# Placing lookup tables on chip, or loading them whole: the tables of the second step of a Fourier-and-MLP kernel

## The chip, the cores and the metric

The kernel runs on one core of one Trainium2 chip. The metric is the device time of one execution in microseconds (us), lower is better. The engines are TensorE (PE; its weight loads are PEld), VectorE (DVE), ScalarE (ACT), GpSimd (POOL) and SyncE (SP, which here only issues transfers). All times inside an execution count from the start of its span. All executions quoted are of the state "fast"; there was no slow one.

## The reference, cut to what matters

```python
X = np.fft.rfft(x, axis=1)                 # x: 8 x 3008 x 256
Yr = Xr @ w_r - Xi @ w_i + b_r ;  Yi = Xr @ w_i + Xi @ w_r + b_i
Yr, Yi = soft_threshold(Yr, 0.01), soft_threshold(Yi, 0.01)
y = np.fft.irfft(Yr + 1j * Yi, n=3008, axis=1)
h = np.maximum(y.reshape(-1, 256) @ w_in, 0.0)        # 256 -> 2048
out = (s * h * h + b) @ w_out                         # 2048 -> 256
```

The transform of length 3008 = 94 x 32 is done as two DFT steps, each a matrix product with a table. The second step takes 24 pairs of frequencies, each with its own 128 x 128 block-structured table: `F_t` and `F_2` forward (for the real and imaginary part of the mixed input), `T_t` inverse.

## The kernel before

The kernel first takes batch 0 through the transform alone; after that it runs the MLP of one batch beside the transform of the next, and TensorE is full (10.00 busy in 80 to 90 us). The change touches batch 0 only. There, half of each table is zero, so the tables arrive compact (`F_c`, `T_c`), the full tiles are zeroed, and VectorE and ScalarE copy the blocks into place.

```python
H = NPAIR // 2                     # 12 of 24 pairs
F_c = uspool.tile([P, NPAIR, 2, N2], F16)          # compact forward tables
T_c = uspool.tile([P, NPAIR, 64], F16)             # compact inverse table

def emit_load_forward():           # issued early in the input's loading
    nc.sync.dma_start(out=F_c[:, 0:H], in_=F_d[:, 0:H]); ...
def emit_load_inverse():           # issued when the input is nearly through
    nc.sync.dma_start(out=F_c[:, H:], in_=F_d[:, H:])
    t_load = nc.sync.dma_start(out=T_c, in_=T_d)
    ...                            # identity, last table, biases, scalars

nc.vector.memset(F_t, 0.0); nc.vector.memset(T_t, 0.0)
for f in F_2: nc.gpsimd.memset(f, 0.0)

def place_f(h):      # ScalarE: 2 copies of 64 x 768
    for a in range(2): nc.scalar.copy(out=blocks(F_t)[r, q, :, a], in_=F_c[r, q])
def place_f_2(h):    # VectorE: 4 operations of 64 x 384, two of them with a sign
    ...
def place_t(h):      # VectorE: 4 copies of 32 x 768
    for i in range(4): nc.vector.tensor_copy(out=T_t[r, q, c : c + 64], in_=T_c[r, q])

# ... first DFT step of batch 0 (products with x, evictions ut) ...
place_f(0); place_f_2(0)
gate = nc.gpsimd.tensor_copy(out=w_in_t[0][0:1, 0:1], in_=T_c[0:1, 0, 0:1])
# behind the gate on GpSimd: loads of batch 1's input, of w_in and of w_out
for i in range(2 * U + 2):         # U = 6; 12 steps, pipelined
    mix(...)        # TensorE x8, then eviction g (VectorE in 2 of 3 steps, ScalarE in 1)
    fwd_dft(...)    # TensorE x8 with F_t and F_2; m (ScalarE), then z (VectorE)
    inv_dft(...)    # TensorE x4 with T_t; eviction vt
    if i == 0: place_t(0)
    if i == 1: place_f(1)
    if i == 2: place_f_2(1)
    if i == 3: place_t(1)
```

A one-element memset ahead of each load holds the load back until the right eviction is done: in the trace the memset for `F_c` runs at 8.37 us, behind an eviction ut, and the load is issued at 8.48.

## Time and profile before

| | before |
|---|---|
| time | 851.64 us, median of 3 (851.37 to 852.25) |
| span of the profiled execution | 849.4 us |
| first forward product of batch 0 | 17.14 us |
| sixth forward product | 27.46 us |
| first product of the MLP (with `w_in`) | 49.59 us |
| from there to the end | 799.8 us |

The two ends of what follows, from the TensorE timeline:

```profile
17.14 0.22 PE L441 MATMUL psf<-g,F_t 128*128 128x128 f16 x1 [0.55 <-DVE g L420]
...
27.46 0.22 PE L441 MATMUL psf<-g,F_t 128*128 128x128 f16 x1
```

"First forward product" is the first TensorE product with `F_t`; each step makes eight such products with `F_t` and `F_2`. The time from the first to that of the sixth step is what I call **the stretch**: it holds the placing copies that the change removes (the first of them starts at 17.00, just before it), it is 10.32 us here, and TensorE's own work in it is about 8.0, an estimate that the prediction works out from the trace.

### The profile page before, as it was taken

To read this page: it belongs to the slowest core of one execution; us is meant where nothing else is said; L and a number is where in the kernel's file an instruction comes from. 1 tells how busy PE (TensorE), PEld (TensorE's weight loads), DVE (VectorE), ACT (ScalarE), POOL (GpSimd) and SP (SyncE) were. 2 spreads that over 40 slices of the span, in tenths; PEclk is the share of its full clock that TensorE was granted. 3 is DMA by queue.
4 is the path that set the end of the run, shared out by engine and by line. 5 is a ranking of instruction groups with operands and counts; after the bars stand their busy time and mean duration, and the time that the engine had idled before them with its cause. 6 is when DMAs were issued, how large, how long until landed. Compare 5 with 4: busy or idle time off the path is not lost.

```text
span 849.4 us, 17085 instructions
## 1 busy us (share of the span) xinstructions
PE 835.0 (98%) x6645; PEld 600.5 (71%) x6645; DVE 697.0 (82%) x1027; ACT 643.2 (76%) x856; POOL 46.6 (5%) x72
## 2 busy tenths in 40 slices
PE   8899999999999999999999999999999999999997
PEld 7757777777677766777677776777667777766765
DVE  6898987888888987888878888888977888776674
ACT  5898887787778787787777887787877787766673
POOL 5321000000000000000000000000000000000000
PEclk9999999999999999999999999999999999999999
DMA  7937457324761367324662247613354223411111
GB/s 165 161 104 162 108 148 185 101 76 100 177 186 54 92 159 184 109 78 103 171 177 65 74 106 199 172 40 92 100 156 118 62 79 98 112 33 38 38 44 50
DMA packets 105458, 95.07 MB, mean 112 GB/s; under 512 B 9510, under 2 KB 97578, under 8 KB 104034
## 3 DMA queue, kind: packets, MB, share of 16 engines
q1 hardware_dynamic: 98930, 79.57, 32.6%
q0 software_dynamic: 6448, 14.42, 10.7%
q8 instruction: 52, 0.85, 0.4%
q14 instruction: 28, 0.23, 0.1%
HBM read 52.54 MB, written 46.66 MB: 117 GB/s over the span
## 4 chain that ended last, share of the span: by engine, by line
PE 88%; DVE 4%; ACT 3%; DMA 2%; issue 1%; POOL 0%; SPq 0%; DVEq 0%; ACTq 0%; POOLq 0%
PE psa L832 36%; PE psh L761 36%; PE psf L627 4%; PE psf L562 2%; PE psf L613 2%; PE psf L598 2%; PE psf L657 2%; PE psf L710 2%; ACT rt L768 1%; DVE gt L775 1%; DMA x<-in_x_dram 1%; DMA out_dram<-ost 1%; PE psh L410 1%; ACT yt L160 0%; ACT vs L160 0%
## 5 line engine op out<-in xcount | busy, mean ns | idle before, releaser
L768 ACT ACTIVATE rt<-psh 128x1024 f32<-128x1024 f32 (+2 forms) x384 | 387.1, 1009 | 119.1 <-PE psh L761 117.7
L775 DVE TENSOR_TENSOR gt<-rt 128x1024 f16<-128x1024 f32 (+2 forms) x321 | 384.0, 1199 | 98.1 <-ACT rt L768 97.4
L832 PE MATMUL psa<-w_out_t,gt 128*128 128x256 f16 (+1 forms) x3024 | 454.3, 272 | 0.1
L832 PEld LDWEIGHTS <-gt 128*128 128x128 f16 (+1 forms) x3024 | 300.9, 101 | 187.2 <-issue 1.7
L761 PE MATMUL psh<-yt,w_in 128*128 128x512 f16 (+1 forms) x1344 | 396.7, 378 | 0.3 <-ACT rt L768 0.3
L761 PEld LDWEIGHTS <-w_in 128*128 128x128 f16 x1536 | 142.9, 98 | 27.4 <-issue 2.1
L842 DVE SCALAR_TENSOR_TENSOR ost<-psa,s_bc,bias_bc 128x512 f32<-128x512 f32 (+2 forms) x97 | 71.0, 732 | 8.3 <-PE psa L832 7.1
L772 ACT ACTIVATE gt<-rt 128x1024 f16<-128x1024 f32 (+2 forms) x63 | 66.2, 1050 | 1.0
L632 DVE TENSOR_TENSOR ring<-psf,s 128x512 f16<-128x512 f32 x84 | 57.5, 684 | 3.7 <-PE psf L627 2.9
L160 ACT CAST v<-psf 128x512 f16<-128x512 f32 x78 | 45.3, 582 | 18.7 <-PE psf L657 18.7
L160 ACT CAST xf<-psf 128x512 f16<-128x512 f32 x82 | 47.9, 585 | 10.9 <-PE psf L598 10.8
L160 ACT CAST u<-psf 96x512 f16<-96x512 f32 x77 | 44.5, 580 | 11.0 <-PE psf L562 10.7
L761 PE MATMUL psh<-tail,w_in 128*128 128x512 f16 (+1 forms) x192 | 52.1, 353 | 0.0
L627 PE MATMUL psf<-W_g,xf 128*128 128x256 f16 x336 | 50.4, 273 | 0.0
L160 ACT CAST yt<-psf 128x480 f16<-128x480 f32 (+2 forms) x75 | 38.1, 520 | 13.6 <-PE psf L710 13.6
L189 POOL DMA_DIRECT2D x<-in_x_dram x36 | 18.9, 530 | 429.3 <-PE psf L562 428.0
L562 PE MATMUL psf<-x,A_t 94*96 94x512 f16 x104 | 39.7, 381 | 1.7 <-ACT yt L160 0.5
L638 DVE TENSOR_TENSOR ring<-ring,high 128x512 f16<-128x512 f16 x84 | 35.5, 423 | 2.3
L639 DVE TENSOR_TENSOR ring<-ring 128x512 f16<-128x512 f16 x84 | 35.5, 422 | 1.9
L637 DVE TENSOR_TENSOR ring<-ring,low 128x512 f16<-128x512 f16 x84 | 35.4, 421 | 1.6
L627 PEld LDWEIGHTS <-xf 128*128 128x128 f16 x336 | 32.9, 98 | 3.8
L710 PE MATMUL psf<-C_t,vs 96*128 96x96 f16 x448 | 33.0, 205 | 0.1
(89 smaller groups left out, 501.9 us busy)
## 6 DMA issues: line engine op xcount, KB each, us to landing
out_dram<-ost SPq DMA_DIRECT2D x152, 128.0 KB
ud<-u SPq DMA_DIRECT2D x28, 384.0 KB
us<-ud SPq DMA_DIRECT2D x28, 384.0 KB
vd<-v SPq DMA_DIRECT2D x42, 256.0 KB
vs<-vd SPq DMA_DIRECT2D x14, 768.0 KB
x<-in_x_dram POOLq DMA_DIRECT2D x28, 376.0 KB, 5.9
ring<-ring SPq DMA_DIRECT2D x280, 32.0 KB
out_dram<-ost SPq DMA_DIRECT2D x16, 120.0 KB
```

The costliest lines, as they stand in the source:

```text
L160: return None, nc.scalar.copy(out=dst, in_=src)
L562: nc.tensor.matmul(ps[0:96, :], A_t[0:N1, :], x16[(b, c)][0:N1, j * D : (j + 2) * D], start=True, stop=True,)
L627: nc.tensor.matmul(ps[:, r, :], xt[:, 2 - r, dc], W_g[:, dc, r], start=(dc == 0), stop=(dc == DC - 1),)
L632: nc.vector.tensor_tensor(out=t, in0=ps, in1=hold[i // 2][:, i % 2].unsqueeze(1).to_broadcast([P, 2, D]), op=ALU.add,)
L638: nc.vector.tensor_tensor(out=m, in0=m, in1=high, op=ALU.min)
L710: nc.tensor.matmul(ps[:, j * 96 : (j + 1) * 96], vs[(b, h)][:, k, ec * P : (ec + 1) * P], C_t, start=True, stop=True,)
L761: nc.tensor.matmul(o, w_in_t[dc][:, mc * P : (mc + 1) * P], r, start=(dc == 0), stop=(dc == DC - 1),)
L768: nc.scalar.activation(out=rt[:, :, 0:w], in_=ps[:, :, 0:w], func=AF.Relu)
L772: nc.scalar.activation(out=gt[:, :, 0:w], in_=rt[:, :, 0:w], func=AF.Square)
L775: nc.vector.tensor_tensor(out=gt[:, :, 0:w], in0=rt[:, :, 0:w], in1=rt[:, :, 0:w], op=ALU.mult)
L832: nc.tensor.matmul(ps[0:size, h, :], gts[(ti, mc // 2)][:, mc % 2, sub * size : (sub + 1) * size], w_out_t[:, mc, :], start=(mc == 0), sto ...
L842: nc.vector.scalar_tensor_tensor(out=ost[0:size, 0:k], in0=ps[0:size, 0:k], scalar=s_bc[0:size], in1=bias_bc[0:size, 0:k], op0=ALU.mult, o ...
```

## The change

The intent is to take the copies off VectorE and ScalarE, where the first batch waits for them, and to let transfers bring the tables ready-made. It costs 983,040 more bytes. The first half of the forward tables is still placed, because it is needed first and the compact form is small.

```diff
-    F_d = nc.inline_tensor(fwd.astype(np.float16), name="dft_fwd").ap()
-    T_d = nc.inline_tensor(inv.astype(np.float16), name="dft_inv").ap()
+    F_d = nc.inline_tensor(fwd[:, 0:H].astype(np.float16), name="dft_fwd").ap()
+    ...                       # f_d, f_2_d, t_d: the same tables with their zeros, built beforehand
     def emit_load_inverse():
-        nc.sync.dma_start(out=F_c[:, H:].rearrange(...), in_=F_d[:, H:])
-        t_load = nc.sync.dma_start(out=T_c, in_=T_d)
+        nc.sync.dma_start(out=T_t[:, 0:H], in_=t_d[:, 0:H])
+        nc.sync.dma_start(out=F_t[:, H:], in_=f_d)
+        nc.sync.dma_start(out=F_2[1], in_=f_2_d)
+        t_load = nc.sync.dma_start(out=T_t[:, H:], in_=t_d[:, H:])
-    nc.vector.memset(F_t, 0.0)
-    nc.vector.memset(T_t, 0.0)
-    for f in F_2:
-        nc.gpsimd.memset(f, 0.0)
+    nc.vector.memset(F_t[:, 0:H], 0.0)
+    nc.gpsimd.memset(F_2[0], 0.0)
-        gate = nc.gpsimd.tensor_copy(out=w_in_t[0][0:1, 0:1], in_=T_c[0:1, 0, 0:1])
+        gate = nc.gpsimd.tensor_copy(out=w_in_t[0][0:1, 0:1], in_=F_t[0:1, H, 0:1])
-            if i == 0: place_t(0)      # (each behind the step's eviction g)
-            if i == 1: place_f(1)
-            if i == 2: place_f_2(1)
-            if i == 3: place_t(1)
```

More of the change, by code (lines that the diff above doesn't have):

```diff
@@ L123 @@
     A_d = nc.inline_tensor(first.astype(np.float16), name="dft_first").ap()
-    F_d = nc.inline_tensor(fwd.astype(np.float16), name="dft_fwd").ap()
-    T_d = nc.inline_tensor(inv.astype(np.float16), name="dft_inv").ap()
+    F_d = nc.inline_tensor(fwd[:, 0:H].astype(np.float16), name="dft_fwd").ap()
+    f_all = np.zeros((P, NPAIR, 2, 2, N2))
+    t_all = np.zeros((P, NPAIR, 2, 64))
+    for i in range(4):
+        r = slice(32 * i, 32 * i + 32)
+        f_all[r, :, :, i // 2] = fwd.reshape(P, NPAIR, 2, N2)[r]
+        t_all[r, :, i % 2] = inv[r]
+    f_2 = np.stack([-f_all[:, H:, 1], f_all[:, H:, 0]], axis=2)
+    f_d, f_2_d, t_d = (
+        nc.inline_tensor(t.reshape(P, -1, P).astype(np.float16), name=name).ap()
+        for t, name in ((f_all[:, H:], "fwd_rest"), (f_2, "fwd_rest_i"), (t_all, "dft_inv"))
+    )
     C_d = nc.inline_tensor(last.astype(np.float16), name="dft_last").ap()
@@ L220 @@
             nc.sync.dma_start(out=b_g[r : r + 1, i], in_=bv.unsqueeze(0))
-    F_c = uspool.tile([P, NPAIR, 2, N2], F16, name="F_c", tag="us")
+    F_c = uspool.tile([P, H, 2, N2], F16, name="F_c", tag="us")
+    F_2 = [uspool.tile([P, H, P], F16, name="F_2", tag="us") for _ in range(2)]
     b_h = cpool.tile([P, D], F16, name="b_h")
@@ L227 @@
     sel_t = cpool.tile([P, P], F16, name="sel_t")
-    T_c = uspool.tile([P, NPAIR, 64], F16, name="T_c", tag="us")
     eye_t = cpool.tile([P, P], F16, name="eye_t")
@@ L237 @@
     bb_bc = cpool.tile([P, 1], F32, name="bb_bc")
+    F_t = cpool.tile([P, NPAIR, P], F16, name="F_t")
+    T_t = cpool.tile([P, NPAIR, P], F16, name="T_t")
     def emit_load_forward():
         nc.sync.dma_start(
-            out=F_c[:, 0:H].rearrange("p q r k -> p q (r k)"), in_=F_d[:, 0:H]
+            out=F_c.rearrange("p q r k -> p q (r k)"), in_=F_d
         )
@@ L245, in emit_load_inverse @@
     def emit_load_inverse():
-        nc.sync.dma_start(
-            out=F_c[:, H:].rearrange("p q r k -> p q (r k)"), in_=F_d[:, H:]
-        )
-        t_load = nc.sync.dma_start(out=T_c, in_=T_d)
+        nc.sync.dma_start(out=T_t[:, 0:H], in_=t_d[:, 0:H])
+        nc.sync.dma_start(out=F_t[:, H:], in_=f_d)
+        nc.sync.dma_start(out=F_2[1], in_=f_2_d)
+        t_load = nc.sync.dma_start(out=T_t[:, H:], in_=t_d[:, H:])
         with tc.issue_after(t_load.ins):
@@ L271 @@
     nc.vector.memset(neg_lam, -LAM)
-    F_t = cpool.tile([P, NPAIR, P], F16, name="F_t")
-    nc.vector.memset(F_t, 0.0)
-    T_t = cpool.tile([P, NPAIR, P], F16, name="T_t")
-    nc.vector.memset(T_t, 0.0)
-    F_2 = [uspool.tile([P, H, P], F16, name="F_2", tag="us") for _ in range(2)]
-    for f in F_2:
-        nc.gpsimd.memset(f, 0.0)
+    nc.vector.memset(F_t[:, 0:H], 0.0)
+    nc.gpsimd.memset(F_2[0], 0.0)
     def make_bounds():
@@ L298, in place_w, with place_f, place_f_2 @@
             nc.scalar.copy(out=W_t[:, :, i], in_=w_st[i])
-    def place_f(h):
-        q = slice(h * H, h * H + H)
+    def place_f():
         for a in range(2):
             r = slice(64 * a, 64 * a + 64)
-            nc.scalar.copy(out=blocks(F_t)[r, q, :, a], in_=F_c[r, q])
-    def place_f_2(h):
-        q = slice(h * H, h * H + H)
+            nc.scalar.copy(out=blocks(F_t)[r, 0:H, :, a], in_=F_c[r])
+    def place_f_2():
         for a in range(2):
@@ L311, in place_f_2 @@
             nc.vector.tensor_scalar_mul(
-                out=blocks(F_2[h])[r, :, 0, a], in0=F_c[r, q, 1], scalar1=-1.0
+                out=blocks(F_2[0])[r, :, 0, a], in0=F_c[r, :, 1], scalar1=-1.0
             )
-            nc.vector.tensor_copy(out=blocks(F_2[h])[r, :, 1, a], in_=F_c[r, q, 0])
-    def place_t(h):
-        q = slice(h * H, h * H + H)
-        for i in range(4):
-            r = slice(32 * i, 32 * i + 32)
-            c = 64 * (i % 2)
-            nc.vector.tensor_copy(out=T_t[r, q, c : c + 64], in_=T_c[r, q])
+            nc.vector.tensor_copy(out=blocks(F_2[0])[r, :, 1, a], in_=F_c[r, :, 0])
     w_sum = cpool.tile([P, D], F16, name="w_sum")
@@ L382, in first_batch @@
                 with tc.issue_after(last_dve.ins):
-                    nc.vector.memset(F_c[0:1, H, 0, 0:1], 0.0)
-                    nc.vector.memset(T_c[0:1, 0, 0:1], 0.0)
+                    for t in (T_t[:, 0:H], F_t[:, H:], F_2[1], T_t[:, H:]):
+                        nc.vector.memset(t[0:1, 0, 0:1], 0.0)
                 emit_load_inverse()
@@ L389, in first_batch @@
         with tc.issue_after(last_dve.ins), tc.issue_after(last_act.ins):
-            place_f(0)
-            place_f_2(0)
-        gate = nc.gpsimd.tensor_copy(out=w_in_t[0][0:1, 0:1], in_=T_c[0:1, 0, 0:1])
+            place_f()
+            place_f_2()
+        gate = nc.gpsimd.tensor_copy(out=w_in_t[0][0:1, 0:1], in_=F_t[0:1, H, 0:1])
         with tc.issue_after(gate.ins):
@@ L402, in first_batch @@
         zt = {}
-        g_last = [None]
         def mix(ec, u):
@@ L416, in mix @@
             if u % 3 == 1:
-                g_last[0] = nc.scalar.copy(out=g, in_=ps)
+                nc.scalar.copy(out=g, in_=ps)
                 load["act"] += 1.02
             else:
-                g_last[0] = nc.vector.tensor_tensor(
+                nc.vector.tensor_tensor(
                     out=g, in0=ps,
@@ L523, in first_batch @@
                 some(3)
-            if i == 0:
-                with tc.issue_after(g_last[0].ins):
-                    place_t(0)
-            if i == 1:
-                with tc.issue_after(g_last[0].ins):
-                    place_f(1)
-            if i == 2:
-                with tc.issue_after(g_last[0].ins):
-                    place_f_2(1)
-            if i == 3:
-                with tc.issue_after(g_last[0].ins):
-                    place_t(1)
             if i == 9:
```

## The prediction

> **What bounds the kernel now.** I read the page's busy line first and then its chain of waits by engine.
>
> ```profile
> PE 835.0 (98%) x6645; PEld 600.5 (71%) x6645; DVE 697.0 (82%) x1027; ACT 643.2 (76%) x856; POOL 46.6 (5%) x72
> ...
> PE 88%; DVE 4%; ACT 3%; DMA 2%; issue 1%; POOL 0%; SPq 0%; DVEq 0%; ACTq 0%; POOLq 0%
> ```
>
> TensorE is the bound over the whole, and the 12% of the chain that is not TensorE is where a change off TensorE can act. The view by stretches (columns: PE, PEld, DVE, ACT, POOL busy us, clock, DMA share, GB/s) shows where that is.
>
> ```profile
> 10.00:20.00 10.00, 8.95 (x113) 7.84 (x111) 7.52 (x18) 8.19 (x14) 3.69 (x8) 0.90 0.70 162
> 20.00:30.00 10.00, 8.31 (x100) 6.72 (x98) 9.41 (x17) 7.44 (x12) 1.66 (x2) 1.00 1.04 205
> 30.00:40.00 10.00, 9.51 (x133) 8.46 (x131) 8.24 (x11) 8.53 (x15) 5.74 (x7) 1.00 1.04 158
> ...
> 80.00:90.00 10.00, 10.00 (x82) 7.59 (x81) 9.12 (x20) 9.14 (x14) 0.00 (x0) 1.00 0.33 87
> ```
>
> From about 57 us on TensorE is full. In the first batch it is not: in 20 to 30 us TensorE is idle for 1.7 us and VectorE is the fullest engine, 9.4 of 10. The tables of the second DFT step are placed just there, so this stretch decides. Next I read the timeline of VectorE in it.
>
> ```profile
> 15.86 1.22 DVE L420 TENSOR_TENSOR g<-psh,b_g 128x1024 f16<-128x1024 f32 x1 [0.26 <-PE psh L410]
> 17.00 1.52 DVE L321 COPY T_t<-T_c 32x768 f16<-32x768 f16 x4
> 18.66 1.23 DVE L420 TENSOR_TENSOR g<-psh,b_g 128x1024 f16<-128x1024 f32 x1
> 19.80 0.68 DVE L448 SCALAR_TENSOR_TENSOR z<-psf,m 128x512 f16<-128x512 f32 x1
> 20.68 0.69 DVE L448 SCALAR_TENSOR_TENSOR z<-psf,m 128x512 f16<-128x512 f32 x1 [0.20 <-ACT m L446]
> 21.29 0.45 DVE L311 TENSOR_SCALAR F<-F_c 64x384 f16<-64x384 f16 x1
> 21.66 0.23 DVE L314 COPY F<-F_c 64x384 f16<-64x384 f16 x1
> 21.91 0.26 DVE L311 TENSOR_SCALAR F<-F_c 64x384 f16<-64x384 f16 x1
> 22.09 0.26 DVE L314 COPY F<-F_c 64x384 f16<-64x384 f16 x1
> 22.38 1.23 DVE L420 TENSOR_TENSOR g<-psh,b_g 128x1024 f16<-128x1024 f32 x1
> 23.52 0.68 DVE L448 SCALAR_TENSOR_TENSOR z<-psf,m 128x512 f16<-128x512 f32 x1
> 24.11 1.44 DVE L321 COPY T_t<-T_c 32x768 f16<-32x768 f16 x4
> 25.58 0.69 DVE L448 SCALAR_TENSOR_TENSOR z<-psf,m 128x512 f16<-128x512 f32 x1
> ```
>
> The copies stand back to back with the evictions g and z that TensorE needs. On TensorE the timeline has the matching hole, a wait of 1.28 us for g, and on ScalarE two placing copies stand ahead of the activations m:
>
> ```profile
> 23.65 0.22 PE L441 MATMUL psf<-g,F_t 128*128 128x128 f16 x1 [1.28 <-DVE g L420]
> ...
> 17.66 0.83 ACT L304 COPY F_t<-F_c 64x768 f16<-64x768 f16 x1
> 18.40 0.68 ACT L446 ACTIVATE m<-psf,neg_lam 128x512 f32<-128x512 f32 x1
> 19.10 0.83 ACT L304 COPY F_t<-F_c 64x768 f16<-64x768 f16 x1
> 19.96 0.69 ACT L446 ACTIVATE m<-psf,neg_lam 128x512 f32<-128x512 f32 x1
> ```
>
> [...] The trace has 0.34 to 0.44 us for one, so I use the trace. [...] the trace reached 331 GB/s in 15 to 16 us, when these tables stream in. [...]
>
> **The change part by part.** Removed from VectorE: eight inverse-table copies (1.52 and 1.44 us) and four of the forward table (21.29 to 22.35, 1.06 us), together 4.0 us; also one and a half memsets of 1.34 us before 5 us, where VectorE waits for input anyway (1.05 us idle before the first eviction): worth nothing. Removed from ScalarE: two copies of 0.83 us. Removed from GpSimd: one of two memsets (2.71 us for both), done by 10.74, 4 us before use: worth nothing. Added: two 0.06 us gate memsets in a VectorE gap, and bytes. Before, half of F_c (196,608) and T_c (393,216) are 589,824 bytes; after, four transfers of 393,216 make 1,572,864: 983,040 more.
>
> What lies on the path, replaying the trace's durations:
> - Copies at 17.00: g before them ends at 17.08, and the next g needs a mix product that TensorE finishes at 18.62. They fill a wait; removal gives about 0.
> - ScalarE copies: without the second, m starts at 19.28, when its product is there, not 19.96. Its z then starts at 20.40, when the z before it lets VectorE go, not 20.68: 0.28 us.
> - Forward copies: g (22.38) then follows z directly, at 21.0: 1.06 plus 0.28 plus 0.04 = 1.38 us. The product after it moves from 23.65 to about 22.25.
> - Copies at 24.11: z (25.58) now waits not for them but for its m. The product ends at 22.9, but ScalarE is in the g of step 4 until about 23.2, so m runs 23.2 to 23.9 and z starts at about 23.9: 1.7 us early. So of these 1.44 us only 0.3 is new.
> - From there the line is full: the next g moves from 26.19 to about 24.5, the product of step 5 from 27.46 to about 25.7, that of step 6 from 29.18 to about 27.5. All are about 1.7 us earlier.
>
> Sum: 5.7 us of work leaves two engines, 1.7 us leaves the path. A floor checks it: TensorE's own work per step is 0.87 (mix) + 0.44 (forward) + 0.22 (inverse) + a third of 0.22, about 1.6 us, so the five steps from 17.14 to 27.46 (10.3 us) cannot fall below 8.0, and the gain cannot pass 2.3 us. Later work depends on the first batch and on transfers issued from it; after 57 us TensorE is full and keeps the lead. So 851.64 - 1.7 = 849.9, rounded to 849.8 because an order of VectorE that takes the first z ahead of g could gain a little more.
>
> **The rivals.** (1) The loads take the place of the copies: TensorE would wait for a table. The bytes of the present loads are through near 16.0 us (244 GB/s in 14 to 15, 331 in 15 to 16) and the gate that waits for them runs here:
>
> ```profile
> 16.72 0.18 POOL L393 COPY w_in<-T_c 1x1 f16<-1x1 f16 x1 [5.97 <-DMA T_c<-dft_inv]
> ```
>
> That is 0.7 us for completion. At 331 GB/s, as estimates from those rows, the four new loads land at about 16.2, 17.3, 18.5 and 19.7 us. They are needed, in the faster schedule, at 20.5 (first half of T_t), 22.2 (F_t and F_2) and 24.6 (rest of T_t). Each has over 3 us. If I am wrong here by a factor of two in rate, the wait is 1 to 3 us and the gain is lost or turned to a loss of 1 us.
> (2) The transfers behind the gate come late. The gate now waits for the second load, 17.3, so 0.6 us later; its first packets came some 2.4 us after the gate, so at about 19.7, as the tables end. The second batch's input is needed at 42.8, far off. The tightest is w_out: landed at 39.6, summed on GpSimd until 48.96, used by a product at 56.36 (54.7 after). One microsecond later is absorbed; it would take 5. A miss stalls TensorE directly.
> (3) The gain is eaten before 57 us: ScalarE or a PSUM buffer becomes the bound of the first batch, or the order of instructions shifts. In 30 to 40 us ScalarE is 8.5 busy and TensorE 9.5, so neither has room to lose much, but a different interleaving may move the end by some tenths either way. Full loss gives 851.6.
> (4) It gains what was removed, 4.0 us or more: 847.6. Against it: the copies at 17.00 are hidden, and TensorE's floor.
>
> **Range and chances.** Main case, gain 1 to 2.5 us: 70%; gain mostly lost (0 to 1): 18%; over 2.5: 7%; slower: 5%. The runs of before spread 0.9 us. Hence 848.5 to 851.3 for 8 in 10. Two per cent is 17 us, four times all the work removed; a slowdown of 17 us would need a table or weight late by more than the whole load takes. So within 2% is nearly certain.
>
> **What would show it.** Right: in the changed trace VectorE has no table copies after 17 us, its busy time falls by about 6 us (2 of it memsets) and ScalarE's by 1.7; TensorE's 1.28 us wait for g shrinks to near zero; the product of step 5 starts near 25.7; the first product with w_in, at 49.6 now, starts near 47.9; the stage after 57 us is as long as before. The gate runs near 17.3. Wrong: a TensorE wait for F_t, F_2 or T_t ended by a transfer, a wait for w_sum near 55 us, or the 1.7 us present at 27 us and gone at 49.

The sum came to 1.7 us: 0 for the copies at 17.00, 0.28 for those on ScalarE, 1.06 and 0.04 for the forward copies on VectorE, and 0.3 for the copies at 24.11. Read from the trace of the kernel before: one placing copy of 32 x 768 takes 0.34 to 0.44 us, and the transfers reach 331 GB/s in 15 to 16 us.

## The result, and the profile after

The changed kernel takes 849.18 us, the median of 4 runs (849.03 to 849.75), beside 851.71 us for the kernel before on the same occasion. The ratio of the two is 0.9971 with a 95% interval of 0.9954 to 0.9988. Ratios here are the mean time of one kernel's fast runs over that of the other's fast runs of the same rounds, so not quite the ratio of the medians. The forecast was 849.8 in 848.5 to 851.3.

The page of the changed kernel, its busy line and its chain by engine:

```profile
PE 833.7 (98%) x6645; PEld 598.8 (71%) x6645; DVE 691.5 (82%) x1016; ACT 641.2 (76%) x854; POOL 45.6 (5%) x71
...
PE 87%; DVE 4%; ACT 3%; DMA 3%; issue 2%; SPq 0%; POOL 0%; DVEq 0%; ACTq 0%; POOLq 0%
```

VectorE has lost 5.5 us of work and ScalarE 2.0. In the chain the share of transfers is up from 2% to 3%: the load of `F_c` is in it now, with 5.4 us from 9.06 on, and two transfers of the MLP phase, but none of the four new loads. The view by stretches of ten microseconds (columns as in the prediction):

```profile
10.00:20.00 10.00, 8.29 (x105) 6.67 (x106) 6.39 (x17) 7.11 (x12) 2.17 (x5) 1.00 0.87 246
20.00:30.00 10.00, 9.77 (x119) 8.17 (x117) 7.57 (x10) 8.18 (x14) 2.37 (x4) 1.00 0.93 183
```

In 20 to 30 us TensorE is now 9.77 busy (it was 8.31) and VectorE only 7.57 (it was 9.41): the bound of the stretch has moved from VectorE to TensorE. The timeline of VectorE shows the same instruction by instruction (start, duration, engine, line, operation, what it waited for):

```profile
14.59 0.25 DVE L318 TENSOR_SCALAR F<-F_c 64x384 f16<-64x384 f16 x1 [0.68 <-DMA F_c<-dft_fwd]
...
15.49 1.22 DVE L419 TENSOR_TENSOR g<-psh,b_g 128x1024 f16<-128x1024 f32 x1
18.13 0.69 DVE L447 SCALAR_TENSOR_TENSOR z<-psf,m 128x512 f16<-128x512 f32 x1 [1.42 <-ACT m L445]
18.74 1.21 DVE L419 TENSOR_TENSOR g<-psh,b_g 128x1024 f16<-128x1024 f32 x1
19.87 0.68 DVE L447 SCALAR_TENSOR_TENSOR z<-psf,m 128x512 f16<-128x512 f32 x1
20.47 1.22 DVE L419 TENSOR_TENSOR g<-psh,b_g 128x1024 f16<-128x1024 f32 x1
21.60 0.68 DVE L447 SCALAR_TENSOR_TENSOR z<-psf,m 128x512 f16<-128x512 f32 x1
23.55 0.69 DVE L447 SCALAR_TENSOR_TENSOR z<-psf,m 128x512 f16<-128x512 f32 x1 [1.27 <-ACT m L445]
```

No placing copy is left on VectorE after 15.5 us, and VectorE now waits 1.42 and 1.27 us where copies stood. Also, z of the first step (18.13) now runs ahead of the second g (18.74), where before the g came first: the order of the program changed with the copies. TensorE and GpSimd, from their timelines:

```profile
16.77 0.22 PE L440 MATMUL psf<-g,F_t 128*128 128x128 f16 x1 [1.09 <-DVE g L419]
...
18.88 0.40 PE L458 MATMUL psa<-T_t,z 128*128 128x128 f16 x4
...
21.73 0.22 PE L440 MATMUL psf<-g,F_t 128*128 128x128 f16 x1
...
25.43 0.22 PE L440 MATMUL psf<-g,F_t 128*128 128x128 f16 x1
```

```profile
17.49 0.18 POOL L393 COPY w_in<-F_t 1x1 f16<-1x1 f16 x1 [8.42 <-DMA F_t<-fwd_rest]
...
41.43 1.15 POOL L327 TENSOR_TENSOR acc<-w_out_t 128x512 f32<-128x512 f16 x1 [5.25 <-DMA w_out_t<-in_moe_w_out_dram]
```

The product of the fourth step starts at 21.73 with no wait (before: 23.65 after 1.28 us). The one forward product that still waits for g, 1.09 us, is the first, and its wait goes back to the transfer of `F_c` (the 0.68 us at 14.59). The first inverse product, at 18.88, waits for no table. The gate opens at 17.49. The weights `w_out` are there at 41.4 instead of 39.6 us.

By landmarks, where the time went between the traces. "Before, second" is another trace of the same kernel, from the experiments:

| | before | before, second | after |
|---|---|---|---|
| first forward product | 17.14 | 17.52 | 16.77 |
| the stretch (to the sixth) | 10.32 | 10.12 | 8.66 |
| sixth forward product to first MLP product | 22.13 | 22.13 | 22.02 |
| first MLP product to the end | 799.8 | 799.8 | 799.8 |
| span | 849.4 | 849.6 | 847.2 |

The stretch gave 1.46 to 1.66 us, the start before it 0.37 to 0.75, and everything after it 0.1.

### The profile page after: what moved, and what is told of

Read it like the earlier page. It is cut to its first block, busy times and chain, and to the rows that moved or that the text cites. A ratio compares the mean times of both kernels' runs of the same rounds, so it can differ in the third digit from the quotient of the medians.

```text
span 847.2 us, 17072 instructions
## 1 busy us (share of the span) xinstructions
PE 833.7 (98%) x6645; PEld 598.8 (71%) x6645; DVE 691.5 (82%) x1016; ACT 641.2 (76%) x854; POOL 45.6 (5%) x71
## 4 chain that ended last, share of the span: by engine, by line
PE 87%; DVE 4%; ACT 3%; DMA 3%; issue 2%; SPq 0%; POOL 0%; DVEq 0%; ACTq 0%; POOLq 0%
PE psa L819 36%; PE psh L748 35%; PE psf L614 4%; PE psf L549 2%; PE psf L600 2%; PE psf L585 2%; PE psf L644 2%; PE psf L697 2%; ACT rt L755 1%; DVE gt L762 1%; DMA out_dram<-ost 1%; DMA x<-in_x_dram 1%; DMA us<-ud 1%; DMA F_c<-dft_fwd 1%; PE psh L409 1%
## 5 line engine op out<-in xcount | busy, mean ns | idle before, releaser
L171 ACT CAST xf<-psf 128x512 f16<-128x512 f32 x82 | 47.9, 585 | 10.9 <-PE psf L585 10.9
```

What stands on the lines that cost most here:

```text
L171: return None, nc.scalar.copy(out=dst, in_=src)
```

## The experiments

**Theory:** what counts is where a copy lies in the chain of g, m and z: copies on that chain cost their time, copies that fill a wait cost nothing, and the larger loads are hidden with some microseconds to spare. **Rival A:** the gain goes by the work removed, zeroings included. **Rival B:** the loads are not hidden, and each further byte costs. Twelve kernels ran, in three calls, each call on one chip with its own runs of the kernel before. Some executions have a few microseconds at half TensorE clock (shown below), which go with longer times (the run of e1 at a mean clock of 0.996 took 853.18 us, the four others at 0.999 or more 850.53 to 851.03); the stretch is free of that in every trace here, because none of the slow clock fell into it.

| run | median us (runs) | ratio to before, 95% interval | first product | stretch |
|---|---|---|---|---|
| e0 before again | 851.53 (5) | 0.9997 (0.9985 to 1.001) | 17.52 | 10.12 |
| e1 only inverse whole | 850.89 (5) | 0.9989 (0.9976 to 1.0001) | 17.15 | 9.87 |
| e2 only forward whole | 849.51 (5) | 0.9972 (0.9958 to 0.9985) | 16.85 | 8.85 |
| e3 zeroings back | 849.78 (5) | 0.9975 (0.9962 to 0.9987) | 18.54 | 8.65 |
| e4 after again | 849.42 (5) | 0.9973 (0.9961 to 0.9985) | 16.82 | 8.65 |
| e5 zeroings back, second | 850.70 (5) | 0.9986 (0.9974 to 0.9998) | 20.02 | 8.66 |
| e6 all whole, early | 850.09 (5) | 0.9983 (0.9970 to 0.9996) | 17.62 | 8.66 |
| e7 1.57 MB ahead | 851.37 (6) | 1.0004 (0.9988 to 1.0019) | 16.86 | 9.49 |
| e8 all whole, late | 851.18 (6) | 0.9994 (0.9981 to 1.0008) | 16.67 | 9.78 |
| e9 ScalarE copies back | 849.84 (5) | 0.9978 (0.9966 to 0.9990) | 17.26 | 8.90 |
| e10 0.79 MB ahead | 851.31 (5) | 0.9992 (0.9980 to 1.0005) | 17.80 | 9.34 |
| e11 zeroings back, third | 850.10 (5) | 0.9981 (0.9969 to 0.9993) | 17.31 | 8.66 |

e0 to e3 ran in the first call (before 851.98 us, 9 runs), e4 to e7 in the second (851.73, 11 runs), e8 to e11 in the third (851.87, 11 runs). All outputs were correct.

### e0 and e4: both kernels again

No edit.

> A control: the kernel before once more, with a second trace. It should come out at a ratio of 1.000 and about 851.7 us. What it is for: in the first trace of before, the start of the first batch (up to the first forward product at 17.14 us) ran with a halved TensorE clock from 9 to 12 us and lost 0.37 us to the changed kernel's. If that is chance of one execution, this trace has another clock there or another start; the stretch from the first forward product (17.14) to the sixth (27.46), 10.3 us, must stay within 0.1 us.

> A control: the changed kernel once more, so that the three others have it on their own chip. About 849.2 us, 2.3 us under the kernel before; the stretch from the first to the sixth forward product 8.7 us as in its first trace (10.1 to 10.3 in the two traces of before).

The control came out at 0.9997. Its stretch is 10.12 us, 0.2 below the first trace's, so my 0.1 us for the spread of the stretch was too tight. Its start is later (17.52), although its clock was full, so the halved clock of the first trace does not explain the later start of the kernel before. The changed kernel repeated at 849.42 us with a stretch of 8.65, within 0.01 us of its first trace. A second reading of e4 is the clock. The view by microsecond of e4 (the third number from the end is the granted clock):

```profile
42.00:43.00 1.00, 1.00 (x7) 0.55 (x7) 0.70 (x2) 0.94 (x2) 0.92 (x2) 1.00 0.00 0
44.00:45.00 1.00, 1.00 (x12) 1.00 (x11) 0.49 (x1) 0.35 (x1) 0.94 (x1) 0.50 0.69 176
47.00:48.00 1.00, 1.00 (x20) 0.88 (x19) 0.71 (x2) 0.73 (x1) 0.92 (x2) 1.00 0.70 180
```

For some 3.4 microseconds the clock is 0.50. In e4 this cost 1.0 us (first MLP product at 48.51 instead of 47.45), in an execution of 850.19 us among others at 849.2 to 849.9. Of the 14 traces nine have such stretches in their first 62 us: that of the first run of the kernel before, e3, e5, e7, e9, e10 and e11 between 7 and 19 us, ahead of the first forward product (only in e5 later than 16 us), and e2 and e4 at 43 to 47 us. The granted clock stands at 1.00 or 0.50, and each of these stretches lasts about 3.4 us, or 6.8 in e3; e5 has two of 3.4. What makes the clock fall is not shown by these runs: from 40 to 44 us TensorE was busy for 2.96 us in e4 and in the first trace of the changed kernel alike, and only in e4 did the clock fall.

### e1 and e2: half of the change each

```diff
# e1: from before                              # e2: from after
-  T_d = inv (compact), place_t(0), place_t(1) -  t_d (whole inverse table)
+  t_d loaded whole into T_t                   +  T_d compact, T_t zeroed, place_t(0), place_t(1)
   (forward tables placed as before)              (forward tables whole as after)
```

> Only the inverse table is loaded whole; the second half of the forward tables is still placed by VectorE and ScalarE. My replay (copies on the path count, copies in a wait do not): the first four inverse copies are hidden and the last four carry 0.3 us, so a gain of 0.2 to 0.7 us, about 851.2 us. The rival (the gain goes by the work removed from VectorE, memset of T_t included: 4.3 of some 7 us) gives 1.4 us or more, 850.3 us or less.

> Only the second half of the forward tables is loaded whole; the inverse table is placed by eight VectorE copies as before. Replay: 1.4 us from the forward copies, and the inverse copies fall into waits of VectorE for the activation m (the changed trace has idle times of 1.42 and 1.27 us there), so 1.4 to 2.2 us of gain, about 849.7 us, within 0.6 us of the changed kernel. The rival (gain by work removed): 1.0 us or less, 850.7 us or more.

The edit of e1 is thus the change without its forward part, that of e2 the change without its inverse part. The inverse part alone shortens the stretch by 0.25 to 0.45 us, and the forward part alone by 1.27 to 1.47. In time, e1 gains 1.1 us by medians (851.98 - 850.89), but the runs behind the 851.98 include executions with a half clock. Beside e0's three clean runs (851.36, 851.45, 851.53) e1's four clean runs (850.53 to 851.03, median 850.84) gain 0.6 us, within the expected 0.2 to 0.7 and below the rival's 1.4; e2's three runs at 0.998 or 0.999 (849.37 to 849.51) gain 2.0. The interval of e1 reaches 1.0001, so I lean on the traces. In e2 all eight inverse copies are there, 2.96 us of VectorE work, and its timeline shows where they went:

```profile
16.71 1.44 DVE L328 COPY T_t<-T_c 32x768 f16<-32x768 f16 x4
18.21 0.69 DVE L455 SCALAR_TENSOR_TENSOR z<-psf,m 128x512 f16<-128x512 f32 x1
...
22.28 1.52 DVE L328 COPY T_t<-T_c 32x768 f16<-32x768 f16 x4
23.83 0.69 DVE L455 SCALAR_TENSOR_TENSOR z<-psf,m 128x512 f16<-128x512 f32 x1
```

They fill the two gaps of the changed kernel, 1.42 us before the z at 18.13 and 1.27 us before the z at 23.55. They lengthen the stretch by 8.85 - 8.66 = 0.19 us. So 2.96 us of removed work were worth 0.2 us, and rival A is out for the copies.

### e9: the forward part split

```diff
 # from after
-  nc.sync.dma_start(out=F_t[:, H:], in_=f_d)
+  nc.sync.dma_start(out=F_c[:, H:], in_=F_d[:, H:])   # compact again
+  if i == 1: place_f(1)                               # two ScalarE copies; F_2 and T_t stay whole; F_t is zeroed whole
```

> The changed kernel with the two ScalarE copies of the second half of F_t put back (F_2 and T_t still whole): it splits the forward part. Replay: the ScalarE copies carry 0.3 us and the VectorE copies 1.1 us, so the stretch from first to sixth forward product is 8.8 to 9.2 us (changed: 8.65; before: 10.1 to 10.3) and the kernel is 0.2 to 0.6 us slower than the changed one. Rival: the gain hangs on the ScalarE copies, because they make m late and turn the order of VectorE; then the stretch is 9.7 us or more.

The stretch is 8.90 us, 0.24 over the changed kernel's, and the time 849.84 us. With the copies back the order of before is back as well (g ahead of the first z, z at 19.92 and 20.81), and still the stretch stays short. So of the forward part the two ScalarE copies carry about a quarter of a microsecond, and what is left of e2's 1.27 to 1.47, about 1.1 us, goes to the four VectorE operations; this share is a difference and has no run of its own.

### e3, e5, e11: the zeroings

```diff
 # from after
-  nc.vector.memset(F_t[:, 0:H], 0.0); nc.gpsimd.memset(F_2[0], 0.0)
+  nc.vector.memset(F_t, 0.0); nc.vector.memset(T_t, 0.0); nc.gpsimd.memset(F_2[0], 0.0); nc.gpsimd.memset(F_2[1], 0.0)
```

> The changed kernel with the three zeroings of before put back (T_t and F_t whole on VectorE, the second F_2 on GpSimd); the loads then overwrite them. They run before 11 us in waits for the input. Replay: worth nothing, 849.2 us within 0.4 us. Rival: 2.0 us of VectorE work at the start push the first batch back, 849.9 us or more.

> The changed kernel with the three zeroings put back, a second time: the first run of it had a median of 849.78 against 849.18 of the changed kernel, but on another chip, and its trace fell in an execution with a halved TensorE clock at 9 to 13 us. If the zeroings are worth nothing, it comes within 0.3 us of the changed kernel's second run; if they carry part of the gain, it is 0.5 us or more slower again, with the first forward product later than 16.8 us at full clock.

> The changed kernel with the three zeroings put back, a third time, to have a trace of it at full clock and five more times. If the zeroings are worth nothing, the runs at a mean clock of 0.999 or more come at 849.2 to 849.5 us as the changed kernel's do; if they carry part of the gain, at 849.8 us or more, with F_c landing later than 14.6 us.

This did not come out cleanly. By what was expected, e3 (849.78) fell between "worth nothing" and the rival, e5 (850.70) on the rival's side, and of the three runs of e11 at full clock two on the rival's side and one on mine. The stretch is untouched (8.65, 8.66, 8.66 us). But the 15 runs with the zeroings have a median of 850.03 us (849.30 to 852.39), the 9 of the changed kernel, on two other occasions, 849.34 (849.03 to 850.19). At a mean clock of 0.999 or more, seven runs with them have 849.30 to 850.83, median 849.83 (those of e11 alone: 849.30, 850.10 and 850.83), eight of the changed kernel 849.03 to 849.88, median 849.30. All three traces fell in executions with a half clock at the start, and none of the changed kernel's two did, so I have no trace of the zeroings at full clock. Putting them back costs something between nothing and 0.7 us, not in the stretch. The sign that e11 looked for, `F_c` landing late, is absent: it landed at 14.45, 13.81 and 14.03 us in the three traces and at 14.49 in the changed kernel's (by the landing marks explained under e7 and e10). Nor are the zeroings needed for a half clock, for e7 and e10 have one without them. In two of the traces part of the loss lies after the first MLP product, from where e3 and e11 took 800.2 and 800.1 us instead of 799.8 (e5 799.7, e2 800.2); whether the rest comes with the half clock, from another change of the start, or by chance, is open.

### e7 and e10: the loads made late

```diff
 # from after; n = 6 in e7, 3 in e10
+  early = [gpool.tile([P, 8, P], F16, tag="gt") for _ in range(n)]
   def emit_load_inverse():
+      for t in early:
+          nc.sync.dma_start(out=t, in_=t_d[:, 0:8])    # 262,144 bytes each, never used
```

> The changed kernel with 1,572,864 bytes of idle loads put in the queue ahead of the four tables, at the changed kernel's rate some 5 us more. If the loads have about 2.5 us to spare, as I work out from the trace of the changed kernel (first half of T_t landed near 16.2, needed at 18.9), TensorE waits for T_t near 19 us for some 2.5 us, and the kernel comes out 2 to 3 us slower than the changed one, about 851.8 us: the whole gain is gone. If the loads are hidden far more deeply, nothing changes; if every byte counted, it would already show in the changed kernel.

> Half of the delay of e7: 786,432 bytes of idle loads ahead of the tables, some 2.5 us. If the loads have about 2.5 us to spare, TensorE waits for no table and not for w_sum, and it comes within 0.4 us of the changed kernel, 849.2 to 849.8. If every byte counts, it loses half of what e7 lost, 0.9 us or more.

In e7 TensorE waits for the table, as the theory says, though for less than 2.5 us. From its TensorE timeline, the first inverse product and the later product with `w_sum`:

```profile
21.28 0.61 PE L462 MATMUL psa<-T_t,z 128*128 128x128 f16 x8 [0.47 <-DMA T_t<-dft_inv]
...
55.89 0.27 PE L340 MATMUL psa<-w_sum,ones 128*128 128x256 f16 x1 [0.63 <-POOL w_sum L336]
```

The order of TensorE had changed too (the third forward product now stands ahead of the first inverse one), which is why only 0.83 us of the stretch is lost. A second wait opens at 55.89: everything behind the gate is late, so `w_out` and its sum are. The median is 851.37 us, 2 us over e4's, so the whole gain is gone. The 0.83 us and the second wait, 0.63, make up 1.5 us of it; the rest was not followed. The trace of e7 is its worst execution, 855.67 us: there TensorE once waits 3.1 us for a transfer of the MLP phase, which the other five runs, at 851.1 to 852.3, need not have.

In e10 I expected no loss and was wrong: the first inverse product waits, the stretch grows by 0.7, and the median is 851.31.

```profile
20.79 0.38 PE L462 MATMUL psa<-T_t,z 128*128 128x128 f16 x4 [0.85 <-DMA T_t<-dft_inv]
```

The kept traces say why. They hold sixteen landing marks for each transfer, and the last one is its landing: where TensorE waited for `T_t` in e7, e8 and e10, it went on 0.04 us after it. In the changed kernel the first half of `T_t` landed at 15.46 for its use at 18.88, so it had 3.4 us to spare, and not the 2.5 that I worked out from "near 16.2". `F_t` had 4.4 us (17.36 for 21.73), `F_2` 2.8 (18.94 for 21.79), and the rest of `T_t` 4.4 (19.89 for 24.30); e4 has the same within 0.5 us. TensorE waits for no table in either trace, which puts rival B out for the changed kernel itself. In e10 the loads were issued at 13.85 instead of 12.04 (`F_c`, at 10.14 instead of 9.06, was late ahead of the half clock, which then ran from about 10.6 to 14), and the three idle loads added 3.5 us where I had counted 2.5. `T_t` landed at 20.75, 5.3 us later than in the changed kernel, while its use moved only from 18.88 to 19.94: 3.4 us of slack gone, and 0.85 of wait. In e7 it landed at 21.24, 5.8 us later, for a use at 20.81. Two of the runs at full clock (851.31 and 852.28) are slower than this explains; what they lost is open.

### e6 and e8: one step further

```diff
 # from after: the first half of F_t and F_2 loaded whole too; no placing, no zeroing at all; gate on the first inverse load
-  F_c load, place_f(), place_f_2(), both memsets
+  nc.sync.dma_start(out=F_t[:, 0:H], in_=f_d[:, 0:H])      # e6: where F_c was issued, beside the input
+  nc.sync.dma_start(out=F_2[0], in_=f_2_d[:, 0:H])         # e8: issued with the other tables, first 4 pairs first
```

> One step further than the change: the first half of the forward tables is loaded whole too, so that nothing is placed by VectorE or ScalarE; the gate for the next input waits for the first inverse table. In five of six traces the first forward product waits for the placing of F_c, whose load lands at 14.5 to 15.3 us behind the input. By the rate of the loads once the input is through (0.3 MB in a microsecond from 12.7 us, and 0.7 us to completion), 786,432 bytes land near 16.0 us, so the first forward product starts near 16.1 instead of 16.8 us and the kernel gains 0.3 to 0.8 us over the changed one. Rival: the doubled bytes in front delay the input or the tables behind, and it is no faster or slower.

> All tables loaded whole as in e6, but issued only when the input is nearly through (with the four others, some 12 us), and the quarter that the first products need ahead of the rest. In e6 the tables held up the last piece of the input (first product with it at 14.2 instead of 12.8 to 13.4 us). If that was its only fault, the first piece (262,144 bytes) lands near 14.5 us, the first forward product waits for g alone and starts near 16.0 us instead of 16.8, and the kernel beats the changed one by 0.3 to 0.8 us, about 848.8 us. Rival: the queue now carries 2.36 MB and the tables behind are late, so TensorE waits for T_t or F_2 and nothing is won.

Both failed, each by its rival. In e6 the tables were in time, but the last piece of the input was not:

```profile
14.20 0.34 PE L339 MATMUL psh<-A_t,x 94*128 94x96 f16 x4 [1.04 <-DMA x<-in_x_dram]
```

It came at 12.81 in the first trace of the changed kernel and at 13.36 in e4, and the first forward product at 16.77 and 16.82; here that is 17.62, late by 0.8 us, while the stretch stays 8.66. In e8 the first product came at 16.67, just 0.1 us earlier, and then the inverse table was late, because now 2.36 MB stand in the queue:

```profile
20.10 0.38 PE L434 MATMUL psa<-T_t,z 128*128 128x128 f16 x4 [1.29 <-DMA T_t<-dft_inv]
```

The stretch grew to 9.78 us. The trace of e8 is its slowest execution (853.11 us): it also has a wait of 0.85 us for the sum of `w_out` at 56.27 and one of 1.4 us for a transfer of the MLP phase. No version that I tried beats the changed kernel, and e2 comes within noise of it. In these two attempts the first tables were better placed on chip, because with their loads the input came late (e6: a wait of 1.04 us, the first product with its last piece at 14.20) or the tables behind them did (e8: a wait of 1.29 us).

## Why the prediction was right

- **The bound and the stretch** were right. TensorE's wait of 1.28 us is gone, TensorE went from 8.31 to 9.77 busy in 20 to 30 us, and the stretch shrank by 1.66 us (1.46 against the second trace of before). The prediction said 1.7.
- **Its terms** were right as well: the forward VectorE copies about 1.1 us (the difference of e2 and e9), the ScalarE copies 0.24 us (e9) for 0.28, the first inverse copies nothing and the last 0.3, together 0.19 us when put back (e2) and 0.25 to 0.45 when taken alone (e1).
- **The order of VectorE** was not as in the replay: the replay kept g ahead of the first z, and the program as built turned them round, which the prediction had named as possible. e9, with the old order, shows that this mattered little.
- **After the stretch** the lead held, as predicted: first MLP product at 47.45 (said: near 47.9), 799.8 us from there as before. VectorE's busy time fell by 5.5 us (said: about 6), ScalarE's by 2.0 (1.7), and the gate ran at 17.49 (17.3).
- **The rival of late loads** was rightly set aside: no table is waited for. The landings were said to be 16.2, 17.3, 18.5 and 19.7 us and were 15.46, 17.36, 18.94 and 19.89. "Each has over 3 us" held for three of the four and not for `F_2`, which had 2.8. For the first half of `T_t` it held by luck, for two errors cancel in part: with z ahead of the second g, TensorE wants that table at 18.88 us and not at 20.5, and the loads were issued 1 us earlier than the replay assumed. The rate of 331 GB/s did not hold (215 GB/s from 16 to 17 us), which took back the early start for the later loads.
- **The tightest transfer** was named rightly, and mis-sized: `w_out` came 1.8 us later (39.6 to 41.4), not 1. Its sum was ready at 50.8 for a use at 54.2. The delay of e7 turned it into a wait.
- **The mis-sized term of the total** is the start: the prediction had no change before the first forward product. It moved from 17.14 (17.52 in the second trace) to 16.77, 0.37 to 0.75 us, which is about the difference between the predicted gain of 1.8 and the measured one: 2.5 by the medians (851.71 - 849.18), 2.2 between clean executions (e0's 851.45 and about 849.2 for the changed kernel). With 2.5 us the gain lies at the very edge of the main case, 1 to 2.5. What sets this start is the transfer of `F_c`, for which ScalarE and VectorE wait 0.53 to 1.23 us in the changed kernel, in e0, e1 and e2 (not in the first trace of before, where it landed at 14.02, ahead of the end of the last evictions ut at 14.58 and 14.83; the clock there had been 0.50 from 8.5 to 11.9). ScalarE in e0 and in the changed kernel:

```profile
15.33 1.67 ACT L304 COPY F_t<-F_c 64x768 f16<-64x768 f16 x2 [1.04 <-DMA F_c<-dft_fwd]
```

```profile
14.57 1.67 ACT L312 COPY F_t<-F_c 64x768 f16<-64x768 f16 x2 [0.91 <-DMA F_c<-dft_fwd]
```

Fifteen of its sixteen landing marks are there at 13.74 us in e0 and 13.32 in the changed kernel; the last comes 1.5 and 1.2 us after them. Why it is late, and why less so after the change, is not shown. While the input was loading, its queue moved nearly everything: in 9 to 12 us, with `F_c` (196,608 bytes) issued from SP at 9.06 and pending, GpSimd's queue moved 0.59 MB in 352 packets and SP's 0.01 MB in 9 (changed kernel); `F_c` landed, at 14.49, only when the input was through (first product with its last piece at 12.81). With longer rows in e6, 3,072 bytes instead of 1,536, SP's queue still moved only 0.06 MB in 10 to 12 us, and yet the first product with the input's last piece came at 14.20 instead of 12.81 to 13.36. Whether SP's queue had pieces ready to move by then is not shown. A rival that no run isolates is the layout of this load: the last mark is at 14.49 to 14.58 in the changed kernel, e2, e4 and e7, where `F_c` is loaded whole, and at 14.87 to 15.24 in e0, e1 and e9, where it is a slice; but it is at 14.02 in the first trace of before, a slice too.

## What to carry to other kernels

Before removing work from an engine, replay the stretch from the timeline and ask, for each instruction, what the engine would do in its place; here 5.7 us of copies were worth about 1.5 us, and four short operations, 1.06 us standing between z and the next g, were most of it. Transfers were a free replacement here as long as they had slack (2.8 us for the tightest table; in e10, where the loads were made late, TensorE waited 0.85 us for one), so read the landing of each against its use. Loads delayed on purpose show what happens past that, but they also move the uses, so their waits alone do not give the slack. Loading one more table whole won nothing in two attempts. Compare landmarks inside the traces, not only total times, where the total scatters by as much as the effect.
